# Attention and two MLPs on one core: the bias of the exponential from one VectorE operation, two loads on another queue, and a new order

## The chip, the cores and the metric

The kernel runs on one core of a Trainium2 chip. The metric is the device time of one launch, in microseconds (us). The kernel before was timed in three runs: 570.5, 571.86 and 574.29 us, median 571.86.

The core has five engines with an instruction queue each: TensorE (PE in the rows, with its weight loads as PEld), VectorE (DVE), ScalarE (ACT), GpSimd (POOL) and SyncE (SP, which here only issues DMA transfers). An engine works through its queue in order; between engines there are semaphores.

## The reference, cut to what matters

```python
q_rot, k_rot = rotate(q), rotate(k)          # 2 x 8 heads, 576 rows, 64 columns; cos/sin tables
scores = q_rot @ k_rot.T / sqrt(64)
scores = scores - max(scores, axis=-1)
attn = exp(scores)
attn = attn / (sum(attn, axis=-1) + 1e-9)
x = attn @ v                                 # heads side by side: 1152 tokens x 512
h = x @ w_in;  g = h * tanh(softplus(h));            y = g @ w_out     # 2048 wide
h = y @ w_in2; g = h * sigmoid(1.702 * h);           out = g @ w_out2  # 2048 wide
```

All of it is float32. The weights arrive as 64-bit floats.

## The kernel before, in words

The program has two parts. The first is attention, over 8 pairs of heads (4 for each of the 2 batch entries); the second is the two MLPs, whose matmuls follow one another without a pause. The change touches only the first part.

To keep float32 precision, numbers are split in a high and a low part, and products take three terms. For a pair, the rows 0 to 511 of q and k are rotated (`rope_ops`, two multiplications for each of q and k, on VectorE or GpSimd), transposed on TensorE (`turn`), and split by ScalarE (`high`) and VectorE (`low`) into the tile `qk`. The rows 512 to 575 of all four pairs of a batch entry lie in one tile, `rest`, and go through `rest_ops`. The scores of a pair are 9 tiles of 128 rows by 576 columns in PSUM, `st`, in a ring of three buffers. A score tile then goes through this chain:

- `s_max` (VectorE): the negated maximum of each row, into `nm[:, 0:1]`;
- `s_bias` (VectorE or ScalarE, as the planner chooses): `nm[:, 1:2] = nm[:, 0:1] * SCALE + LOGP`. LOGP is the logarithm of 2^14, by which the exponentials are scaled;
- `s_exp` (ScalarE): the exponential with that bias, and its row sum. The row sum is a second instruction, an accumulator read;
- a split into two float16 parts (`high`, `low`), and a transpose by DMA or on TensorE (`et`, which uses the same ring as `st`);
- the product with v on TensorE (`pv`), and a normalization (`xf`, `xh`, `xl`).

For v the greatest absolute value of each row is needed first: `v_max` (ScalarE), two activations with accumulator reads for two pairs of heads, whose main output goes to a tile that nobody reads, `junk`.

The order in which all this is issued is made by a planner when the program is built (class `Plan`): each step has a cost for each engine that may run it, the names that it needs and makes, the buffers that it holds, and a rank (`RANK`); the planner plays the program and takes the ready step of the lowest rank. It knows the buffers that it was told of, and `junk` is not among them. Where it sees TensorE waiting more than 0.2 us it puts matmuls whose result nobody uses (`keep_clock`, 128 x 192 in float16, called fillers below) in front of the next step. The order is thus fixed at build time, and the fillers too.

Of the kernel before, what the change touches and what calls it, by code (L numbers as in the profile page):

```python
# [11 lines left out]
F32 = mybir.dt.float32  # L12
# [3 lines left out]
AF = mybir.ActivationFunctionType  # L16
# [6 lines left out]
def kernel(  # L23
# [67 lines left out]
    idle = const.tile([128, 192], F16, name="idle")  # L91
    rtmp = {}
    rest = att.tile([128, 2, 2, NPAIR, 64], F32, name="rest", bufs=1)
    diag = att.tile([128, 2, NPAIR, 128], F32, name="diag", bufs=1)
# [20 lines left out]
    def load_rest(b, i, a):  # L115

        src = (q, k)[i][b].rearrange("(j a) s d -> a s j d", a=2)[a, MAIN:S]
        SP.dma_start(out=rest[64 * a:64 * a + 64, 0, i], in_=src)
# [65 lines left out]
    def rest_ops():  # L184

        s, t = (rest[:, j].rearrange("p i j d -> p (i j) d") for j in range(2))
        n = 2 * NPAIR
# [18 lines left out]
    def turn(p, m):  # L206
# [17 lines left out]
        else:  # L224
            PE.matmul(out=ps[:, 0:64], lhsT=diag[:, 1, p % NPAIR], rhs=pair_id, start=True, stop=True)
            PE.transpose(ps[:, 64:192], diag[:, 0, p % NPAIR], ident)
# [42 lines left out]
    def s_exp(p, n, st, nm):  # L269
# [3 lines left out]
        if (p, n // 2) not in ebuf:  # L273
# [5 lines left out]
            bias=nm[:, 1:2], scale=SCALE, accum_out=sums[p][:, n:n + 1],  # L279
# [366 lines left out]
    class Plan:  # L646
# [13 lines left out]
        PORT = {"rope", "rest", "high", "low", "v low", "xh", "xl", "w", "rr", "rw"}  # L660
# [149 lines left out]
        "rw": 2013.3, "rw DVE": 485.6, "rw POOL": 1292.9, "first": 282.5, "load q": -135.2, "load k": -17.6,  # L810
        "load rest": -720, "load v": 154.6, "load w": 1000.9, "rest": 437.3, "rope": -637.8, "turn": 410.7,
        "v max": 1129.4, "v high": -570.9, "v low": -441.3, "s": -323.6, "max": -880.6, "exp": -420.6,
        "high": -670.9, "low": -495.5, "pt": -314.5, "rc": 499.4, "rr": 1336.6, "rm": 157.8, "rb": 415.9,
        "pv": 512.1, "xf": 156.1, "xh": 414.9, "xl": 588.5, "w": 439.2, "u": -539.4, "rest DVE": 394.7,
        "rope POOL": -724, "high DVE": -1076.2, "low DVE": 586.6, "xh DVE": 489.8, "xl DVE": 503.9, "et": -283.5,
        "eh": 244.8, "el": 413.7, "v high ACT": 551.2, "w POOL": 477, "rr ACT": -503.1, "rr DVE": 449.3,
        "eh DVE": 489.8, "load sin": -726, "load cos": -435.1, "bias": 84, "bias ACT": 1271.3,
# [25 lines left out]
    def plan_rest(b):  # L843
        base, hold = 9 * NPAIR * b, [("rest", b)]
        for i in range(2):
            for a in range(2):
                add("SP", 0.65, (base, "load rest"), lambda i=i, a=a: load_rest(b, i, a), makes=("rest", b), holds=hold,
                    move=0.18, lead=1.2)
        ops = rest_ops()
        made = [("rest", b), "sin", "cos"]  # L850
        for j, f in enumerate(ops + ops[2:]):
            arg = (j - 2,) if j > 1 else ()
            add(None, dict(POOL=1.22, DVE=0.6), (base + j, "rest"), lambda eng, f=f, arg=arg: f(eng, *arg), needs=made,
                makes=("rest", b, j), holds=hold + [("diag", b)] * (j > 1))
            made = [("rest", b, j) for j in range(min(j, 1) + 1)]
# [15 lines left out]
    def plan_pair(p):  # L871
# [8 lines left out]
        for m in range(3):  # L880
            if m < 2:
                need, src = [("sw", p, m), ("st", p, m), "ident"], [("rtmp0", 2 * p + m), ("rtmp1", 2 * p + m)]
            else:
                need, src = [("rest", p // NPAIR, 2), ("rest", p // NPAIR, 3), "ident"], [("diag", p // NPAIR)]
# [28 lines left out]
        for at, n in enumerate(TILES[p]):  # L913
# [6 lines left out]
            else:  # L920
# [102 lines left out]
    add("SP", 0.48, (0, "load sin"), lambda: SP.dma_start(out=rsin.rearrange("p t d -> p (t d)"), in_=rope[:, 0:NSIN]),  # L1023
        makes="sin", move=0.46, lead=1.1)
    add("SP", 0.48, (0, "load cos"), lambda: SP.dma_start(out=rcos.rearrange("p t d -> p (t d)"), in_=rope[:, NSIN:]),
# [129 lines left out]
```

## Time and profile before

| | |
|---|---|
| runs before | 570.5, 571.86, 574.29 us; median 571.86 |
| the profiled execution | 572.92 us, of which its span is 571.1 |
| TensorE busy | 556.7 us, 97% of the span; fillers (L643) 292 matmuls |
| VectorE, ScalarE, GpSimd busy | 358.7, 281.5, 104.6 us |
| granted clock, mean | 0.997 |
| first matmul on scores | at 17.0 us |
| first matmul of the MLPs | at 166.3 us |

Busy time of an engine is the time in which at least one of its instructions ran. Matmuls are pipelined, so instructions overlap, and the start of one to the start of the next is less than its duration. Durations of VectorE overlap too, by some 0.07 us. A row of the trace names the line of the kernel, the engine, the operation and the tiles, output before input.

### The profile page before, as it was taken

The page shows a single profiled execution, that of the slowest core. Times are in us where ns is not written, and L with a number is a line of the kernel's source. Part 1 is how long each engine was busy: PE and PEld are TensorE (multiplying, and loading weights), DVE is VectorE, ACT ScalarE, POOL GpSimd, SP SyncE. Part 2 cuts the span into 40 slices and gives each one's busy share as a digit, 9 for nine tenths or more (in the row PEclk, how much of TensorE's full clock was granted, in tenths as well). Part 3 has the DMA queues.
Part 4 walks back from the last instruction along what each step waited for, and adds up shares of the span by engine and source line. Part 5 has one row for each costly group of instructions (what it writes and reads, how often), then busy time and mean ns, then how long its engine had stood idle before and what let it go on. Part 6 is the DMA issues. An engine that isn't in the chain of part 4 may idle for free.

```text
span 571.1 us, 9367 instructions
## 1 busy us (share of the span) xinstructions
PE 556.7 (97%) x3680; PEld 503.0 (88%) x3680; DVE 358.7 (63%) x657; ACT 281.5 (49%) x627; POOL 104.6 (18%) x95
## 2 busy tenths in 40 slices
PE   7889999999999999999999999999999999999997
PEld 7767777677789999999999999999988889998885
DVE  5888998989974977255896737757540237931031
ACT  2578988999855753122576313256520324752000
POOL 0758777666610000000000000000000000000000
PEclk9989999999999999999999999999999999999999
DMA  5497798769651433323443322323320034300032
GB/s 161 121 202 163 181 194 181 163 116 192 139 143 41 147 111 118 103 75 112 147 148 110 109 60 91 111 75 115 106 75 0 10 101 116 106 1 1 0 111 55
DMA packets 109356, 61.62 MB, mean 108 GB/s; under 512 B 75136, under 2 KB 106112, under 8 KB 109312
## 3 DMA queue, kind: packets, MB, share of 16 engines
q1 hardware_dynamic: 109312, 61.03, 40.7%
q8 instruction: 29, 0.48, 0.4%
q14 instruction: 15, 0.12, 0.1%
HBM read 40.96 MB, written 2.36 MB: 76 GB/s over the span
## 4 chain that ended last, share of the span: by engine, by line
PE 87%; DVE 7%; issue 2%; ACT 2%; SPq 1%; DMA 1%; DVEq 0%; ACTq 0%
PE h L534 31%; PE acc L601 15%; PE acc L615 15%; PE st L248 6%; PE pvps L371 5%; PE pvps L534 4%; PE pvps L601 2%; DVE nm L258 2%; PE pvps L615 2%; PE tps L219 2%; PE et L324 2%; ACT e L276 1%; PE pvps L643 1%; DVE rtmp L181 1%; DMA raw<-in_k_dram 1%
## 5 line engine op out<-in xcount | busy, mean ns | idle before, releaser
L534 PE MATMUL h<-x,whl 128*128 128x384 f32 x1008 | 178.6, 335 | 0.0
L534 PEld LDWEIGHTS h<-x,whl 128*128 128x128 f32 x1008 | 174.9, 188 | 0.8 <-issue 0.8
L465 DVE TENSOR_TENSOR whl<-wf,whl 128x512 fp32r<-128x512 f32 x63 | 43.6, 692 | 95.6 <-ACT whl L464 95.6
L615 PE MATMUL acc<-whl,g 128*128 128x512 f32 x384 | 88.9, 389 | 0.0
L601 PE MATMUL acc<-g,whl 128*128 128x384 f32 x504 | 88.6, 334 | 0.0
L601 PEld LDWEIGHTS acc<-g,whl 128*128 128x128 f32 x504 | 87.5, 188 | 0.0
L615 PEld LDWEIGHTS acc<-whl,g 128*128 128x128 f32 x384 | 72.1, 188 | 14.9
L571 DVE TENSOR_TENSOR g<-t,g 128x384 fp32r<-128x384 f32 x96 | 53.0, 553 | 30.1 <-ACT g L581 30.1
L464 ACT ACTIVATE whl<-wf 128x512 fp32r<-128x512 f32 x64 | 40.1, 627 | 59.3 <-DVE wf L483 40.1
L248 PE MATMUL st<-qk 64*128 64x288 f32 (+1 forms) x432 | 59.7, 325 | 2.9 <-ACT e L276 2.7
L295 POOL TENSOR_TENSOR p<-e,p 128x576 f16<-128x576 f32 x43 | 57.5, 1346 | 20.8 <-issue 11.0
L580 ACT ACTIVATE t<-h 128x384 f32<-128x384 f32 x84 | 40.6, 483 | 40.6 <-PE h L534 40.4
L258 DVE TENSOR_REDUCE nm<-st 128x1 f32<-128x576 f32 x72 | 53.1, 749 | 6.8 <-PE st L248 6.0
L248 PEld LDWEIGHTS st<-qk 64*128 64x128 f32 (+1 forms) x432 | 41.4, 186 | 17.1 <-issue 10.8
L581 ACT ACTIVATE g<-t 128x384 fp32r<-128x384 f32 x96 | 50.6, 527 | 3.1
L276 ACT ACTIVATE e<-st,nm 128x576 f32<-128x576 f32 x64 | 46.9, 734 | 3.1 <-DVE nm L265 2.1
L480 DVE SCALAR_TENSOR_TENSOR wf<-wraw,wf 128x512 int32<-128x512 int32 x64 | 45.2, 706 | 1.6
L483 DVE SCALAR_TENSOR_TENSOR wf<-wraw,wf 128x512 int32<-128x512 int32 x64 | 44.1, 689 | 1.3
L371 PE MATMUL pvps<-pt,vh 128*64 128x256 f16 (+1 forms) x480 | 37.9, 293 | 0.0
L371 PEld LDWEIGHTS <-vh 128*64 128x64 f16 x480 | 23.5, 110 | 9.0 <-issue 7.1
L643 PE MATMUL pvps<-idle 128*128 128x192 f16 x292 | 30.2, 255 | 1.0 <-DVE idle L1014 1.0
L1096 DVE TENSOR_TENSOR acc<-acc,acc 128x512 f32<-128x512 f32 x8 | 5.5, 687 | 37.1 <-PE acc L615 37.1
(102 smaller groups left out, 538.8 us busy)
## 6 DMA issues: line engine op xcount, KB each, us to landing
wraw<-in_moe_w_in_dram SPq DMA_DIRECT2D x32, 512.0 KB, 3.5
wraw<-in_moe_w_out_dram SPq DMA_DIRECT2D x32, 512.0 KB, 3.4
raw<-in_v_dram SPq DMA_DIRECT2D x4, 512.0 KB, 5.1
raw<-in_q_dram SPq DMA_DIRECT2D x3, 512.0 KB, 4.0
raw<-in_k_dram SPq DMA_DIRECT2D x3, 512.0 KB, 5.3
out_dram<-acc SPq DMA_DIRECT2D x10, 128.0 KB, 2.4
out_dram<-acc SPq DMA_DIRECT2D x4, 256.0 KB, 2.4
raw<-in_q_dram SPq DMA_DIRECT2D x2, 256.0 KB, 3.2
```

Source lines behind the costliest of these rows:

```text
L248: PE.matmul(out=st[:, g, 0:HALF], lhsT=t[r, ql, c0:c0 + 128], rhs=t[r, kl, KC + HALF * g:KC + HALF * g + HALF], start=(i == 0), stop=(i == 2),
L258: DVE.tensor_reduce(out=nm[:, 0:1], in_=st[:, :, 0:HALF], axis=AX.XY, op=ALU.max, negate=True)
L276: ACT.activation(out=ebuf[p, n // 2][:, n % 2, :].rearrange("p (g s) -> p g s", g=2), in_=st[:, :, 0:HALF], func=AF.Exp, bias=nm[:, 1:2], ...
L295: eng.tensor_tensor(out=t[1], in0=src, in1=t[0], op=ALU.subtract)
L371: PE.matmul(out=ps[64 * a:64 * a + 64, 0:W], lhsT=w[:, vl, a, kb, :], rhs=pt[:, KB * (2 * a + pl) + kb, :], start=(n == 0), stop=(n == len ...
L480: lambda: DVE.scalar_tensor_tensor(out=t, in0=hi, scalar=-0x40000000, in1=t, op0=ALU.bitwise_and, op1=ALU.bitwise_or),
L483: lambda: DVE.scalar_tensor_tensor(out=t, in0=lo, scalar=29, in1=t, op0=ALU.logical_shift_right, op1=ALU.bitwise_or),
L534: PE.matmul(out=ps[:, 0:UN], lhsT=w[:, wl, 128 * kk:128 * kk + 128], rhs=src[:, xl, kk, cols(u)], start=(kk == 0 and (wl, xl) == X_LAST[0] ...
L571: DVE.tensor_tensor(out=gl, in0=t, in1=f32(gh), op=ALU.subtract)
L581: ACT.activation(out=gh, in_=t, func=AF.Copy)
L601: PE.matmul(out=ps[:, 0:UN], lhsT=w[:, wl, 128 * f:128 * f + 128], rhs=g[:, gl, 4 * half + f, cols(u)], start=(half == 0 and f == 0 and (w ...
L615: PE.matmul(out=ps, lhsT=g[:, gl, f, 128 * t:128 * t + 128], rhs=w[:, wl, :], start=(f == 0 and (gl, wl) == TERMS[0]), stop=(f == FC - 1 a ...
```

## The change

It does four things.

- `s_max` and `s_bias` become one `tensor_tensor_reduce`: to each score a constant (`shift`, minus LOGP / SCALE) is added, the sum is multiplied by -SCALE, and the minimum over the row is kept, which is the bias that the exponential wants. The 576 products themselves are written as float16 to `junk`, the tile that `v_max` also writes. The built program has two VectorE instructions for it, the main one and one on `nm` alone.
- The cos and sin tables and the rows 512 to 575 of q and k of the first batch entry are loaded by transfers issued from ScalarE's queue, no longer from SyncE's.
- The tiles `rest` and `diag` are laid out with the pair outermost, and for the first batch entry the pair 0 is computed apart from the pairs 1 to 3.
- `RANK` and a few planner costs are new, so the whole attention part comes in another order.

```diff
-    rest = att.tile([128, 2, 2, NPAIR, 64], F32, name="rest", bufs=1)
-    diag = att.tile([128, 2, NPAIR, 128], F32, name="diag", bufs=1)
+    rest = att.tile([128, 2, NPAIR, 2, 64], F32, name="rest", bufs=1)
+    diag = att.tile([128, NPAIR, 2, 128], F32, name="diag", bufs=1)
...
     def s_max(st):
-        nm = att.tile([128, 2], F32, tag="nm", name="nm", bufs=4)
-        DVE.tensor_reduce(out=nm[:, 0:1], in_=st[:, :, 0:HALF], axis=AX.XY, op=ALU.max, negate=True)
+
+        nm = att.tile([128, 1], F32, tag="nm", name="nm", bufs=4)
+        DVE.tensor_tensor_reduce(
+            out=junk[:, 0:S].rearrange("p (g s) -> p g s", g=2), in0=st[:, :, 0:HALF], in1=shift.unsqueeze(2).to_broadcast([128, 2, HALF]), scale=-SCALE,
+            scalar=3.0e38, op0=ALU.add, op1=ALU.min, accum_out=nm,
+        )
         return nm
-
-    def s_bias(nm, eng):
-        if eng is ACT:
-            ACT.activation(out=nm[:, 1:2], in_=nm[:, 0:1], func=AF.Copy, scale=SCALE, bias=LOGP)
-        else:
-            DVE.tensor_scalar(nm[:, 1:2], nm[:, 0:1], SCALE, LOGP, op0=ALU.mult, op1=ALU.add)
...
-            bias=nm[:, 1:2], scale=SCALE, accum_out=sums[p][:, n:n + 1],
+            bias=nm, scale=SCALE, accum_out=sums[p][:, n:n + 1],
...
-        "rw": 2013.3, "rw DVE": 485.6, "rw POOL": 1292.9, "first": 282.5, "load q": -135.2, "load k": -17.6,
+        "rw": -414.4, "rw DVE": -540.2, "rw POOL": -100, "first": 1741.3, "load q": -421.8, "load k": -518.5,
...
     def plan_rest(b):
         base, hold = 9 * NPAIR * b, [("rest", b)]
+        e, q = (SP, "SP") if b else (ACT, "ACT")
         for i in range(2):
             for a in range(2):
-                add("SP", 0.65, (base, "load rest"), lambda i=i, a=a: load_rest(b, i, a), makes=("rest", b), holds=hold,
+                add(q, 0.65, (base, "load rest"), lambda i=i, a=a: load_rest(e, b, i, a), makes=("rest", b), holds=hold,
                     move=0.18, lead=1.2)
...
+        for j0, j1 in ((0, NPAIR),) if b else ((0, 1), (1, NPAIR)):
+            ops = rest_ops(slice(j0, j1))
...
-            add("DVE", 0.665, (g, "max"), lambda n=n: d.update({("m", n): s_max(d["s", n])}), needs=[("s", g)],
+            add("DVE", 0.72, (g, "max"), lambda n=n: d.update({("m", n): s_max(d["s", n])}), needs=[("s", g)],
                 makes=("max", g), holds=[s_at, ("nm", g)])
-            add(None, dict(DVE=0.069, ACT=0.094), (g, "bias"), lambda eng, n=n: s_bias(d["m", n], eng),
-                needs=[("max", g)], makes=("bias", g), holds=[("nm", g)])
-            add("ACT", 0.717, (g, "exp"), lambda n=n: s_exp(p, n, d["s", n], d["m", n]), needs=[("bias", g)],
+            add("ACT", 0.717, (g, "exp"), lambda n=n: s_exp(p, n, d["s", n], d["m", n]), needs=[("max", g)],
...
+    DVE.memset(shift, -LOGP / SCALE)
...
-    add("SP", 0.48, (0, "load sin"), lambda: SP.dma_start(out=rsin.rearrange("p t d -> p (t d)"), in_=rope[:, 0:NSIN]),
+    add("ACT", 0.48, (0, "load sin"), lambda: ACT.dma_start(out=rsin.rearrange("p t d -> p (t d)"), in_=rope[:, 0:NSIN]),
         makes="sin", move=0.46, lead=1.1)
```

The order changes at many places. Three of them matter for what follows.

The first is the head of SyncE's queue, which issues the first loads (`raw_85` is q, `raw_86` k and `raw_87` v of the kernel before):

```order
L1023 DMA rsin<-in_rope_dram 128x320
L118 DMA rest<-in_q_dram 64x4x64 x2
L118 DMA rest<-in_k_dram 64x4x64 x2
L1025 DMA rcos<-in_rope_dram 128x320
L110 DMA raw_85<-in_q_dram 128x2x256 x2
L110 DMA raw_86<-in_k_dram 128x2x256 x2
L110 DMA raw_87<-in_v_dram 128x4x256
```

In the changed kernel SyncE begins with k, q and v at once (there `raw_87` is k, `raw_86` q and `raw_88` v), and the six small transfers stand at the head of ScalarE's queue, in front of its table load, and `v_max` (L132) has come in front of the first splits (L233):

```order
L1026 DMA rsin<-in_rope_dram 128x320
L1028 DMA rcos<-in_rope_dram 128x320
L119 DMA rest<-in_q_dram 64x4x64 x2
L119 DMA rest<-in_k_dram 64x4x64 x2
L132 ACT_TABLE_LOAD
L132 ACTIVATE junk,vs<-raw_88 128x640 x2
L233 ACTIVATE qk<-tps 128x512 x2
L233 ACTIVATE qk<-pvps 128x192
```

Before, one split stood in front of `v_max`, and two behind it.

The third place is VectorE's queue some 80 rows into the changed program, around the second call of `v_max`. The rows are those of the change, with the engines that each waits for (Activation is ScalarE; a wait for DVE is one for an earlier instruction of the same engine):

```order
L294 TENSOR_TENSOR pr<-er,pr 128x576 [waits DMAHW4_49,DMAHW5_49,Activation_49,Pool_49]
L260 ISA junk,nm<-st,shift 128x576 [waits DVE_49,PE_49]
L260 ISA nm 128x1
L260 ISA junk,nm<-st,shift 128x576 [waits DVE_49,PE_49,Activation_49]
L260 ISA nm 128x1
```

In the program, `v_max` stands between these two uses of `junk`, and on ScalarE it waits for the first of them:

```order
L392 ACTIVATE rb_700<-rps,vs 128x256 [waits PE_49]
L132 ACTIVATE junk,vs<-raw_88 128x640 [waits DMAHW7_49,DMAHW0_49,DVE_49]
L132 ACTIVATE junk,vs<-raw_88 128x640 [waits Activation_49]
L275 ACTIVATE e,sums<-st,nm 128x576 [waits PE_49,Pool_49]
L275 ACTIVATE e,sums<-st,nm 128x576 [waits DVE_49]
```

Before, `L131 ACTIVATE junk` waited for no VectorE instruction that writes `junk`, since there was none, and no `L258 TENSOR_REDUCE` waited for it. Each reduction of a score tile, one instruction before (72 of them, and 40 of the 72 biases on VectorE, 32 on ScalarE), is two now, 144 in all.

Counted over the whole program, the change also issues 209 fillers in place of 292 (of those in front of the first score matmul 65 in place of 93), runs ten rotations fewer on VectorE (eight with cos, two with sin) and ten more on GpSimd, and does three `et` copies, six `xl` subtractions and two `pr` subtractions more on VectorE. Of the `rest` operations VectorE had seven of 512 columns; it now has five, all smaller, and GpSimd has the others. The second, third and fourth call of `v_max` each stand between two uses of `junk` on VectorE; behind the second call the next use follows at once, behind the other two one other VectorE operation of 512 or 640 columns lies between.

## Rows read from the trace of the kernel before

**Rows 1.** Windows: us, busy of PE, PEld, DVE, ACT, POOL; clock; DMA; GB/s.
```profile
0.00:5.00 5.00, 3.99 (x30) 3.81 (x31) 1.71 (x8) 1.28 (x1) 1.38 (x10) 1.00 0.33 79
5.00:10.00 5.00, 3.37 (x37) 2.98 (x36) 2.59 (x4) 0.00 (x0) 0.00 (x0) 1.00 0.93 268
...
300.00:400.00 100.00, 100.00 (x579) 100.00 (x578) 65.62 (x120) 40.44 (x78) 0.00 (x0) 1.00 0.31 96
```

**Rows 2.** Windows, same columns: the start, one stretch, the rest of attention.
```profile
0.00:17.00 17.00, 13.34 (x121) 11.93 (x121) 10.83 (x23) 4.36 (x8) 1.47 (x11) 1.00 0.62 172
...
92.00:110.00 18.00, 17.74 (x166) 12.79 (x165) 16.40 (x33) 16.38 (x43) 14.43 (x14) 1.00 0.81 187
...
17.00:166.00 149.00, 142.25 (x1368) 108.91 (x1368) 134.16 (x253) 126.89 (x327) 102.68 (x85) 0.99 0.77 165
```

**Rows 3.** Windows of the fillers (L643) alone: busy of PE and PEld.
```profile
0.00:17.00 17.00, 9.91 (x93) 9.10 (x93) 1.00 0.62 172
17.00:166.00 149.00, 20.33 (x199) 16.06 (x199) 0.99 0.77 165
```

**Rows 4.** Timeline of PE: start, duration; two blocks of fillers.
```profile
27.81 1.74 PE L643 MATMUL pvps<-idle 128*128 128x192 f16 x19
...
155.05 1.91 PE L643 MATMUL pvps<-idle 128*128 128x192 f16 x21
```

**Rows 5.** Timeline, the start: loads, rotation, v_max, first score matmuls.
```profile
1.19 1.40 SPq L118 DMA_DIRECT2D rest<-in_q_dram  x2
...
4.59 0.95 SPq L110 DMA_DIRECT2D raw<-in_q_dram  x2
...
7.69 0.69 DVE L177 TENSOR_TENSOR rtmp<-raw,rsin 128x512 f32<-128x512 f32 x1 [1.17 <-DMA raw<-in_q_dram]
...
12.70 0.74 ACT L131 ACTIVATE junk<-raw 128x640 f16<-128x640 f32 x1 [1.44 <-DMA raw<-in_v_dram]
...
17.00 1.46 PE L248 MATMUL st<-qk 64*128 64x288 f32 x15
```

**Rows 6.** Groups by form: line, operation, count | busy, mean ns | idle before.
```profile
L258 DVE TENSOR_REDUCE nm<-st 128x1 f32<-128x576 f32 x72 | 53.1, 749 | 6.8 <-PE st L248 6.0 <-ACT e L276 0.2
...
L181 DVE TENSOR_TENSOR rtmp<-raw,rcos 128x512 f32<-128x512 f32 x12 | 11.3, 944 | 0.6 <-PE tps L219 0.6
...
L235 DVE TENSOR_TENSOR qk<-tps,qk 128x512 fp32r<-128x512 f32 x16 | 10.8, 680 | 1.8 <-ACT qk L232 1.8
...
L265 DVE TENSOR_SCALAR nm<-nm 128x1 f32<-128x1 f32 x40 | 5.9, 149 | 0.7
```

**Rows 7.** Timeline of one score tile: reductions, bias, exponential and its accumulator read.
```profile
84.14 1.42 DVE L258 TENSOR_REDUCE nm<-st 128x1 f32<-128x576 f32 x2 [0.27 <-PE st L248]
...
85.59 0.15 DVE L265 TENSOR_SCALAR nm<-nm 128x1 f32<-128x1 f32 x1
85.67 1.02 DVE L156 SCALAR_TENSOR_TENSOR vh<-raw,vs,vh 128x640 f16<-128x640 f32 x1
85.68 0.73 ACT L276 ACTIVATE e<-st,nm 128x576 f32<-128x576 f32 x1
...
86.31 0.20 ACT L276 ACTIVATION_READ_ACCUMULATOR e<-st,nm 128x1 f32 x1
...
86.40 0.74 ACT L276 ACTIVATE e<-st,nm 128x576 f32<-128x576 f32 x1
```

**Rows 8.** Timeline of ScalarE: one call of v_max in mid program.
```profile
99.88 0.72 ACT L131 ACTIVATE junk<-raw 128x640 f16<-128x640 f32 x1
...
101.37 0.19 ACT L131 ACTIVATION_READ_ACCUMULATOR junk<-raw 128x1 f32 x1
```

**Rows 9.** Windows, columns as in Rows 1: a wait of TensorE and its clock.
```profile
36.00:38.00 2.00, 0.70 (x6) 0.56 (x8) 2.00 (x6) 1.30 (x4) 0.00 (x0) 1.00 1.33 155
38.00:40.00 2.00, 2.00 (x18) 1.36 (x16) 1.47 (x3) 2.00 (x6) 1.45 (x2) 0.61 0.93 195
40.00:42.00 2.00, 2.00 (x12) 1.69 (x12) 0.82 (x2) 1.43 (x5) 1.17 (x1) 0.54 1.04 351
```

More of the change, by code (lines that the diff above doesn't have):

```diff
@@ L182, in rope_ops, with rest_ops @@
         return swapped, straight
-    def rest_ops():
-        s, t = (rest[:, j].rearrange("p i j d -> p (i j) d") for j in range(2))
-        n = 2 * NPAIR
+    def rest_ops(js):
+        s, t = (rest[:, i, js].rearrange("p j i d -> p (j i) d") for i in range(2))
+        n = 2 * (js.stop - js.start)
         def swapped(eng):
@@ L224, in turn @@
         else:
-            PE.matmul(out=ps[:, 0:64], lhsT=diag[:, 1, p % NPAIR], rhs=pair_id, start=True, stop=True)
-            PE.transpose(ps[:, 64:192], diag[:, 0, p % NPAIR], ident)
+            PE.matmul(out=ps[:, 0:64], lhsT=diag[:, p % NPAIR, 1], rhs=pair_id, start=True, stop=True)
+            PE.transpose(ps[:, 64:192], diag[:, p % NPAIR, 0], ident)
             c0, c1 = KC + MAIN, QC
@@ L659 @@
         WINDOW, BUSY = 10.24 / 3, 3400
-        PORT = {"rope", "rest", "high", "low", "v low", "xh", "xl", "w", "rr", "rw"}
+        PORT = {"rope", "rest", "first rest", "high", "low", "v low", "xh", "xl", "w", "rr", "rw"}
         def __init__(self):
@@ L809 @@
     RANK = {
-        "rw": 2013.3, "rw DVE": 485.6, "rw POOL": 1292.9, "first": 282.5, "load q": -135.2, "load k": -17.6,
[L811 to L817, printed above, removed]
+        "rw": -414.4, "rw DVE": -540.2, "rw POOL": -100, "first": 1741.3, "load q": -421.8, "load k": -518.5,
+        "load rest": 404.2, "load v": -155.7, "load w": 2071, "rest": -678.3, "rope": 1998.5, "turn": -1992.8,
+        "v max": 2001.6, "v high": 2045.4, "v low": -951.4, "s": -757.6, "max": -587.8, "exp": -419.9,
+        "high": 2428.6, "low": -328.2, "pt": 1223.5, "rc": -411.5, "rr": -87, "rm": -372.7, "rb": 1744.8,
+        "pv": 1873.8, "xf": -1174.7, "xh": -65, "xl": 2152, "w": 2384.5, "u": 1911.9, "first rest": -763.2,
+        "first rest DVE": 208.9, "rest DVE": 2564.8, "rope POOL": -340.4, "high DVE": -485.6, "low DVE": 1853.8,
+        "xh DVE": -672.1, "xl DVE": 1730.2, "et": 16.2, "eh": 1537.4, "el": -884.5, "v high ACT": -85.1,
+        "w POOL": -443.6, "rr ACT": -466.4, "rr DVE": 1995.9, "eh DVE": -583.6, "load sin": -997.5,
+        "load cos": -213.4,
     }
@@ L844, in plan_rest @@
         base, hold = 9 * NPAIR * b, [("rest", b)]
+        e, q = (SP, "SP") if b else (ACT, "ACT")
         for i in range(2):
             for a in range(2):
-                add("SP", 0.65, (base, "load rest"), lambda i=i, a=a: load_rest(b, i, a), makes=("rest", b), holds=hold,
+                add(q, 0.65, (base, "load rest"), lambda i=i, a=a: load_rest(e, b, i, a), makes=("rest", b), holds=hold,
                     move=0.18, lead=1.2)
[L849 to L855, printed above, removed]
+        for j0, j1 in ((0, NPAIR),) if b else ((0, 1), (1, NPAIR)):
+            ops = rest_ops(slice(j0, j1))
+            made, kind = [("rest", b), "sin", "cos"], "rest" if b or j0 else "first rest"
+            n = (j1 - j0) / NPAIR
+            for j, f in enumerate(ops + ops[2:]):
+                arg = (j - 2,) if j > 1 else ()
+                add(None, dict(POOL=0.12 + 1.1 * n, DVE=0.07 + 0.53 * n), (base + j0 + j, kind),
+                    lambda eng, f=f, arg=arg: f(eng, *arg), needs=made,
+                    makes=[("rest", NPAIR * b + k, j) for k in range(j0, j1)], holds=hold + [("diag", b)] * (j > 1))
+                made = [("rest", NPAIR * b + j0, j) for j in range(min(j, 1) + 1)]
     def plan_v(ps):
```

11 lines of the change are left out of this document (6 added, 5 removed).

## The prediction

> **What bounds the kernel now.** I read the windows first, to see where time can be won at all. In the MLPs TensorE is busy all of every 100 us [rows 1], and the change takes nothing from them; only what lies before the first MLP matmul counts, some 166 us. In the first 17 us there is no score matmul; in the other 149 TensorE is busy 142.25, VectorE 134.16 (90%), ScalarE 126.89 (85%) and GpSimd 102.68 [rows 2]. TensorE's figure is too good, so I read the fillers next: 9.91 us of it in the start and 20.33 later are matmuls that nobody needs [rows 3]. The reader should see two kinds of stretch. From 92 to 110 TensorE is busy 17.74 of 18.00 without a filler: there it is the bound itself, and nothing that eases VectorE shows. Elsewhere it waits for VectorE and ScalarE, behind fillers or idle. What can be won is at most fillers and idle time: 30.2 us of fillers and 17.0 - 13.34 + 149.0 - 142.25 = 10.4 us idle. The third view is the timeline: the start, one score tile, and one call of v_max. Real TensorE work is the same after the change, so I count what happens to its waits.
>
> **The start.** SyncE spends 0.65 to 0.7 us on issuing each 64 KB piece of `rest`, and reaches the first load of q only at 4.59 [rows 5]. In these first 5 us the transfers run at 79 GB/s, in the next 5 at 268 [rows 1]: issuing is the limit, not moving. With both queues issuing from the beginning, and some 2 us until the first bytes move, the first 5 us would carry 3 x 268 = 804 KB in place of 5 x 79 = 395, so all that follows lands about 409 / 268 = 1.5 us earlier. v now comes first on ScalarE: v_max began at 12.70 [rows 5] and would begin at about 11.2; it takes 1.68 us from the first activation to the end of the last read [rows 8]. Behind it come two splits of 512 columns and one of 192 with their subtractions, some 2.1 us by the spacings of such operations (680 ns a subtraction [rows 6]). That puts the first score matmul at 15.0, not 17.00: **-2.0 us**. The six transfers on ScalarE cost nothing, since it has only 4.36 us of work in these 17 [rows 2]; were they slow there, the table load behind them would still be done before 11. The bounds: -3.4 if v is no gate (VectorE then has some eight operations of 0.6 between q's landing and the first subtraction), -0.5 if the two queues' transfers delay one another and v lands only little earlier. The order's 28 fillers fewer before the first score matmul say -2.4, inside the bounds.
>
> **The later fillers.** 144 stand behind the first score matmul in place of 199. One costs (1.91 - 1.74) / 2 = 0.085 us [rows 4]; 55 x 0.085 = **-4.7 us**, if the waits that they stood for are gone. So I ask whether the engines are really relieved. VectorE: the new operation reads 576 columns from PSUM and a constant from SBUF and writes float16. Nearest is the subtraction `qk`, also PSUM and SBUF in, 680 ns for 512 columns with no stretching by GpSimd over 16 of them, so about 750 for 576, no more than the reduction's 749 [rows 6]. Reductions start 1.42 - 0.75 = 0.67 apart [rows 7]. The small second instruction is not in the trace on VectorE. Nearest is ScalarE's accumulator read, which starts 0.10 before its parent ends (85.68 + 0.73 against 86.31) and is followed 0.09 later by the next [rows 7]; a bias on VectorE is followed after 0.08. So the pair takes 0.67 + 0.08 = 0.75 by the nearest row. Below it cannot go under 0.67 + 0.06; above, if the read starts as the dependent bias did, 0.03 after the end (84.14 + 1.42 against 85.59), it is 0.75 + 0.03 + 0.08 = 0.86. At 0.75, 72 x 0.08 = 5.8 us come, 40 biases x 0.08 = 3.2 go. Ten rotations go, at 944 ns (stretched, since GpSimd's operations and these hold each other up; I take the sine ones alike): 9.4 us. Seven `rest` operations give way to five smaller, at least 2 x 0.68 = 1.4. Eleven other operations come, each at most as long as a reduction: at most 8.2. VectorE's sum: at most +2.6 - 9.4 - 1.4 + 8.2 = 0, and nearer -3, as most of the eleven are shorter. ScalarE loses 32 biases, some 0.1 each, 3 us, and gets about as much back as half of that. GpSimd gets ten rotations, about 13 us, and gives up as many shorter ones; it had 46 us free [rows 2]. Per tile the step from maximum to exponential is shorter by some 0.15, as no second engine comes between. So the relief is there, small, and about the size of the fillers taken out.
>
> **A new wait.** `junk` ties VectorE and ScalarE together. Around the second call of v_max, VectorE's next use of `junk` stands directly behind the use that v_max waits for: VectorE stops for 1.68 us [rows 8], with all of its later work behind it, and the next tile's exponential waits for that. Around the third and fourth call one operation of about 0.7 lies between, and 1.0 is left. That is at most 1.7 + 1.0 + 1.0 = 3.7. At least 0.3 each, 1.0, because ScalarE has an exponential of 0.73 left to run when v_max ends, and only what the next tile needs beyond it (0.75 + 0.15, and a handover) is lost. I take the middle, **+2.0**. The pair's 0.75 against the 0.72 that the order was laid out for: 72 x 0.03 = 2.2 on VectorE, a quarter on the path: **+0.5**.
>
> The sum against the profiled execution's 572.9: 572.9 - 2.0 - 4.7 + 2.0 + 0.5 = 568.7. The median of the three runs lies 1.1 below that execution, which makes 567.6; I say **568.0**.
>
> **The rivals.**
>
> 1. *The waits on `junk` are covered.* ScalarE and TensorE have other work at these places, so +2.0 becomes nothing. And at 36 to 38 TensorE was busy 0.70 of 2.00 us, after which the granted clock fell to 0.61 and 0.54 for 4 us [rows 9], between its levels of 2.4 and 1.2 GHz; that took 0.78 + 0.92 = 1.7 us. In a new order this wait may not be there. 568.0 - 2.0 - 1.0 = 565. For it: only 1.7 of 166 us hang on the clock, at one place. Against: a new order has its own such place.
> 2. *The fillers go, the waits stay.* 55 fillers fewer with TensorE idle in their place gain nothing, and idle stretches may cost clock, as above. Only the start remains: 571.9 - 2.0 + 1 = 571. For it: 92 to 110 shows TensorE as its own bound, and VectorE's relief is only about 2% of its work.
> 3. *The second queue does not help.* If the transfers of the two queues hold each other up, v lands as late as before: the start gains 0, and the rest -4.7 + 2.0 + 0.5 = -2.2, so 570. Against it: issuing took SyncE 3.9 us of the first 4.6 [rows 5] while little moved [rows 1]. The Trainium skill (DMA: Bandwidth & Descriptors, section Issuing engines are not separate DMA queues) is on this rival's side: issuing from several engines only saves the issuing time, which is usually small against the transfer.
> 4. *Slower: the pair is two full instructions.* If the read starts only when the main instruction has ended and the next only when the read has, a tile costs 0.75 + 0.03 + 0.15 = 0.93, 0.26 more than a reduction now. 72 x 0.26 = 18.7, less the 3.2 of biases: +15.5, while some 3 to 6 go elsewhere. VectorE would have to be busy some 145 of 149 us, and it had 14.8 free, most of it waits that stay. I take half of the +15.5 as time: 568.0 + 7.8 + 3 for the splits and exponentials that come late = 579. It decides from about 0.80 a tile on, where the pair's growth (72 x 0.13, less 3.2) eats what the rotations give back. Against it: the bias after a reduction, and the reads on ScalarE, overlap [rows 7]. The Trainium skill (VectorE: DVE Perf Modes, section The DRAIN you can't avoid) says that the next operation does not start until the pipe is empty, and its Rules for kernel authors advise against fusing for speed, for fewer operations instead; 144 in place of 112 is more. Followed to the letter that gives this rival; the trace disagrees where a `vh` starts 0.07 before the bias in front of it ends, 85.67 against 85.74 [rows 7].
>
> **How the numbers follow.** The forecast has 0.40, its own range 565.8 to 570.4; rival 1 has 0.31, rival 2 0.12, rival 3 0.07, rival 4 0.10. More than 1% faster (about what can be told from no change here) is below 566.1: rival 1 and a sixth of the forecast, 0.31 + 0.07 = 0.38. Within 1%: 0.33 + 0.12 + 0.07 = 0.52. Slower: 0.10. The range, 563.0 to 574.0, leaves out rival 4 and the lower third of rival 1.
>
> **What the changed profile would show.** First score matmul near 15.0, and v_max in front of both splits, from about 11; if v_max starts after 12, the start's term is wrong. The new VectorE operation at 740 to 760 ns, started again 0.75 apart; at 0.80 and more rival 4 is on. VectorE idle for about 1.7 us before a score operation released by ScalarE's `junk` row, once, and 1.0 twice; without these rows the +2.0 falls. TensorE idle from 17 us on no more than 7 to 8 us; more means rival 2. The first MLP matmul would come later than the 4.2 us suggest, since the last products of attention now stand in front of it all; the end is what counts. A clock below 0.9 in any two windows of 2 us would make the prediction wrong by about 1 us each.

## The result, and the profile after

The changed kernel takes 568.14 us (median of 6 runs, 567.39 to 569.08) against 573.34 for the kernel before beside it (6 runs, 570.5 to 574.77). The ratio is 0.9915, interval 0.9891 to 0.9939: 4.9 us faster (the medians lie 5.2 apart). The forecast was 568.0 us, 563 to 574. The sum is right; three of its terms are not, and their errors cancel.

The page of the changed kernel (line, engine, operation, count | busy, mean ns | idle before, by releaser), the new operation and the fillers:

```profile
span 565.2 us, 9206 instructions
...
PE 547.8 (97%) x3597; PEld 497.3 (88%) x3597; DVE 355.3 (63%) x686; ACT 278.4 (49%) x599; POOL 112.8 (20%) x99
...
L260 DVE CUSTOM_DVE_ANT_1 junk<-st,shift 128x576 f16<-128x576 f32 x72 | 54.1, 752 | 10.4 <-ACT junk L132 4.4
...
L642 PE MATMUL pvps<-idle 128*128 128x192 f16 x209 | 24.8, 268 | 2.9 <-DVE xf L402 1.8
```

The profiled execution took 567.39 us. TensorE is busy 547.8 of 565.2, so idle 17.4; before it was 556.7 of 571.1, idle 14.4. Of the 5.9 us between the spans, 5.5 are fillers (30.25 [rows 3], now 24.8), 3.5 are real matmuls that took less time (1.7 of it the clock fall of [rows 9], which this execution does not have), and 3.0 came back as idle time.

Windows of the changed kernel, columns as in [rows 1], and in the second fence the fillers alone, as in [rows 3]:

```profile
0.00:5.00 5.00, 3.98 (x26) 3.79 (x27) 1.72 (x9) 0.00 (x0) 1.38 (x10) 1.00 0.62 186
5.00:10.00 5.00, 4.39 (x38) 4.08 (x36) 3.10 (x5) 0.00 (x0) 0.00 (x0) 1.00 1.08 258
...
0.00:17.00 17.00, 12.22 (x96) 11.09 (x97) 10.90 (x24) 4.47 (x9) 4.65 (x13) 1.00 0.64 170
...
17.00:166.00 149.00, 140.35 (x1360) 108.24 (x1358) 134.32 (x289) 125.41 (x304) 108.11 (x87) 1.00 0.87 165
```

```profile
0.00:17.00 17.00, 8.71 (x65) 7.91 (x65) 1.00 0.64 170
17.00:166.00 149.00, 16.08 (x144) 11.87 (x144) 1.00 0.87 165
```

Against [rows 1, 2]: the first 5 us move 186 GB/s in place of 79, as the prediction had it, yet the start hardly gains. From 17 to 166 VectorE is busy as long as before (134.32 against 134.16), but this window is not the same work: in the changed kernel its last 2.62 us belong to the MLPs. From the first score matmul to the first MLP matmul VectorE is busy 132.15 us now (16.67 to 163.38) and was busy 134.43 before (17.00 to 166.30). TensorE idles 8.65 us in place of 6.75.

The start in the timeline (start, duration; what ended the idle time before), against [rows 5]:

```profile
3.97 1.81 ACTq L119 DMA_DIRECT2D rest<-in_k_dram  x2
...
6.77 1.29 DVE L178 TENSOR_TENSOR rtmp<-raw,rsin 128x512 f32<-128x512 f32 x2 [3.97 <-DMA raw<-in_q_dram]
...
10.73 0.29 DVE L192 TENSOR_TENSOR rest<-rest,rsin 128x128 f32<-128x128 f32 x1 [0.87 <-issue]
...
10.94 1.49 DVE L182 TENSOR_TENSOR rtmp<-raw,rcos 128x512 f32<-128x512 f32 x1
10.94 1.28 ACT L132 ACT_TABLE_LOAD   x1 [10.94 <-DMA raw<-in_v_dram]
11.85 1.71 POOL L182 TENSOR_TENSOR rtmp<-raw,rcos 128x512 f32<-128x512 f32 x1
12.24 0.74 ACT L132 ACTIVATE junk<-raw 128x640 f16<-128x640 f32 x1
12.35 1.35 DVE L196 TENSOR_TENSOR rest<-rest,rcos 128x128 f32<-128x128 f32 x1
...
14.23 0.58 DVE L200 TENSOR_TENSOR diag<-rest 64x128 f32<-64x128 f32 x2
...
14.86 0.43 PE L226 MATMUL pvps<-pair_id,diag 128*128 128x64 f32 x2 [2.97 <-DVE diag L200]
...
16.67 0.96 PEld L249 LDWEIGHTS st<-qk 64*128 64x128 f32 x13 [0.17 <-issue]
```

v lands at 10.94 (forecast: about 11.2). But ScalarE's table load waits for v too, so `v_max` begins at 12.24. And a second gate is shut: the rows of `rest` can be used only at 10.73, after q and k (this row names no releaser; the same row from one queue, in experiment 6, names `rest`), and two of VectorE's operations behind that take 1.49 and 1.35 us while GpSimd works beside them. TensorE stands 2.97 us until `diag` is made. The first score matmul comes at 16.67, 0.3 earlier than before.

The same timeline, VectorE and ScalarE: two tiles of the first pair, and the second call of `v_max`, against [rows 7, 8]:

```profile
18.02 0.75 DVE L260 CUSTOM_DVE_ANT_1 junk<-st,shift 128x576 f16<-128x576 f32 x1
18.69 0.08 DVE L260 DVE_READ_ACCUMULATOR2_ANT nm<- 128x1 f32 x1
18.91 0.76 DVE L260 CUSTOM_DVE_ANT_1 junk<-st,shift 128x576 f16<-128x576 f32 x1
...
44.82 0.08 DVE L260 DVE_READ_ACCUMULATOR2_ANT nm<- 128x1 f32 x1
44.82 0.41 DVE L402 TENSOR_TENSOR xf<-pvps,rb 128x256 f32<-128x256 f32 x1
...
48.12 0.19 ACT L132 ACTIVATION_READ_ACCUMULATOR junk<-raw 128x1 f32 x1
...
48.34 0.76 DVE L260 CUSTOM_DVE_ANT_1 junk<-st,shift 128x576 f16<-128x576 f32 x1 [1.76 <-ACT junk L132]
```

The read starts 0.67 after its parent, and another operation starts with it, so the pair costs no more than the reduction did. Only where the next new operation stands directly behind does it start 0.22 after the read, 0.89 after the one before. It writes the same `junk`, but in the one such gap that the profile puts down to a wait it names the read (`nm`, 0.2 us), so what holds it is open. And VectorE stands 1.76 us until `v_max` has left `junk`; there are three such stops, 4.4 us in all (the group's row above).

### The profile page after: what moved, and what is told of

Same layout as the page of the kernel before. It is cut to its first block, busy times and chain, and to the rows that moved or that the text cites. A ratio compares the mean times of both kernels' runs of the same rounds, so it can differ in the third digit from the quotient of the medians.

```text
span 565.2 us, 9206 instructions
## 1 busy us (share of the span) xinstructions
PE 547.8 (97%) x3597; PEld 497.3 (88%) x3597; DVE 355.3 (63%) x686; ACT 278.4 (49%) x599; POOL 112.8 (20%) x99
## 4 chain that ended last, share of the span: by engine, by line
PE 76%; ACT 2%; DVE 2%; issue 1%; POOL 1%; DVEq 0%
PE h L533 31%; PE acc L600 15%; PE acc L614 15%; PE pvps L533 4%; PE st L249 2%; PE pvps L600 2%; PE pvps L370 2%; PE pvps L614 2%; ACT e L275 1%; DVE pt L294 1%; DVE junk L260 1%; PE rps L386 0%; ACT p L288 0%; PE tps L220 0%; POOL rtmp L182 0%
## 5 line engine op out<-in xcount | busy, mean ns | idle before, releaser
L260 DVE CUSTOM_DVE_ANT_1 junk<-st,shift 128x576 f16<-128x576 f32 x72 | 54.1, 752 | 10.4 <-ACT junk L132 4.4
L249 PE MATMUL st<-qk 64*128 64x288 f32 (+1 forms) x432 | 58.3, 322 | 2.3 <-ACT e L275 1.1
L642 PE MATMUL pvps<-idle 128*128 128x192 f16 x209 | 24.8, 268 | 2.9 <-DVE xf L402 1.8
```

Source lines behind the costliest of these rows:

```text
L249: PE.matmul(out=st[:, g, 0:HALF], lhsT=t[r, ql, c0:c0 + 128], rhs=t[r, kl, KC + HALF * g:KC + HALF * g + HALF], start=(i == 0), stop=(i == 2),
L260: DVE.tensor_tensor_reduce(out=junk[:, 0:S].rearrange("p (g s) -> p g s", g=2), in0=st[:, :, 0:HALF], in1=shift.unsqueeze(2).to_broadcast( ...
```

## The experiments

Each was timed beside the kernel before. That spread from 570.3 to 575.9 us (medians 572.5 to 572.8), the kernels of the new order by 1.3 to 2.4 us each, but 3.9 with `rest` before the tables and 4.5 without later fillers. So kernels of the new order are best compared with each other by their medians, where a few tenths say nothing, and with the kernel before by the ratio. For the profiled executions this table splits the span at the first score matmul:

| kernel | median us | ratio, interval | first score matmul | rest of the span |
|---|---|---|---|---|
| before | 573.34 | 1 | 17.00 | 554.1 |
| changed | 568.14 | 0.9915, 0.9891 to 0.9939 | 16.67 | 548.5 |
| changed, again | 568.43 | 0.9932, 0.9906 to 0.9958 | 17.75 | 549.2 |
| own tile | 565.66 | 0.9885, 0.9855 to 0.9915 | 17.64 | 545.9 |
| early table load | 568.78 | 0.9929, 0.9903 to 0.9955 | 16.54 | 548.3 |
| both of these | 566.08 | 0.9888, 0.9858 to 0.9918 | 16.91 | 546.1 |
| both, v behind `rest` | 566.69 | 0.9904, 0.9881 to 0.9926 | 15.93 | 549.2 |
| both, `rest` before tables | 569.16 | 0.9942, 0.9919 to 0.9965 | 19.64 | 548.8 |
| changed, one queue | 568.84 | 0.9937, 0.9918 to 0.9956 | 17.86 | 548.5 |
| changed, two operations | 568.53 | 0.9940, 0.9919 to 0.9961 | 17.54 | 548.9 |
| two operations, one queue | 569.70 | 0.9961, 0.9944 to 0.9977 | 18.33 | 549.0 |
| before, one operation | 573.23 | 1.0012, 0.9996 to 1.0027 | 17.38 | 553.4 |
| before, second queue | 571.76 | 0.9994, 0.9977 to 1.0010 | 17.34 | 553.9 |
| changed, no later fillers | 574.50 | 1.0031, 1.0011 to 1.0051 | 18.05 | 554.5 |

**1. The changed kernel again.** No edit; it stands beside the next ones.

> The changed kernel once more, as the measure for the three that run beside it. Every theory: 568.1 us, plus or minus 0.8.

568.43 us. Its profiled execution took 569.07, 1.7 more than the first one, with the same order and the same wait. The windows show why: this one (first fence, the window of the wait and what follows), and the first execution (second fence):

```profile
12.00:14.00 2.00, 0.00 (x0) 0.00 (x0) 2.00 (x3) 1.96 (x4) 1.74 (x2) 1.00 0.05 17
14.00:16.00 2.00, 0.95 (x5) 0.80 (x6) 1.96 (x5) 1.20 (x4) 0.00 (x0) 0.62 0.76 253
16.00:18.00 2.00, 2.00 (x11) 1.67 (x11) 1.80 (x3) 0.48 (x2) 1.27 (x1) 0.50 0.72 215
18.00:20.00 2.00, 2.00 (x15) 1.93 (x15) 1.40 (x3) 0.45 (x1) 1.54 (x2) 0.50 0.14 47
```

```profile
14.00:16.00 2.00, 0.95 (x7) 0.73 (x8) 1.96 (x5) 1.24 (x3) 0.00 (x0) 1.00 0.84 252
16.00:18.00 2.00, 2.00 (x22) 1.73 (x20) 1.45 (x4) 0.60 (x1) 1.59 (x2) 1.00 0.71 230
```

TensorE idled 3.20 us here and 2.97 there before `diag`. Here the granted clock then fell to 0.50, 1.2 GHz, and was back by 22 us; there it stayed at 1.00, 2.4 GHz.

**2. The new operation's products in a tile of their own.**

```diff
-    junk = att.tile([128, 2 * KB * 64], F16, name="junk", bufs=1)
+    junk = att.tile([128, 2 * KB * 64], U8, name="junk", bufs=1)
+    waste = att.tile([128, S], U8, name="waste", bufs=1)
...
-            out=junk[:, 0:S].rearrange("p (g s) -> p g s", g=2), ...
+            out=waste.rearrange("p (g s) -> p g s", g=2), ...
```

> The changed kernel, but the products of the new VectorE operation go to a tile of their own, so that it and v_max no longer wait for one another; to make room both throw-away tiles hold 8-bit numbers. Order and fillers are the same. Theory A (the prediction's +2.0): VectorE's three waits for v_max (4.4 us in the changed kernel) are gone and 1.0 to 3.7 us come back, about 2, so some 566. Rival (the waits lie beside other work): the three waits are gone and the time is the same within 0.5 us. In both, the new operation stays at 740 to 760 ns.

565.66 us, 2.8 less than the changed kernel beside it, and with the early table load of the next experiment 566.08 against 568.78, again 2.7. The same place in the timeline of this kernel:

```profile
45.55 0.08 DVE L262 DVE_READ_ACCUMULATOR2_ANT nm<- 128x1 f32 x1
45.55 0.41 DVE L404 TENSOR_TENSOR xf<-pvps,rb 128x256 f32<-128x256 f32 x1
...
47.22 0.08 DVE L262 DVE_READ_ACCUMULATOR2_ANT nm<- 128x1 f32 x1
47.44 0.76 DVE L262 CUSTOM_DVE_ANT_1 waste<-st,shift 128x576 uint8<-128x576 f32 x1
```

The stop of 1.76 us is gone; 0.22 behind the read stay, where one such operation directly follows another. The operation takes 752 ns as before, so the smaller products did nothing, and what was won is the wait. This is the best kernel measured, 0.9885 of the kernel before.

**3. The table load early.** One activation on one column behind the six transfers, so that the table is there when v lands.

```diff
+    warm = const.tile([128, 1], F32, name="warm")
...
+        if eng is ACT and i and a:
+            ACT.activation(out=warm, in_=idle[:, 0:1], func=AF.Abs)
```

> The changed kernel with one more ScalarE activation of one column, right behind the six transfers on its queue, so that the table load (1.28 us) is done before v lands. Theory A (ScalarE is the gate of the start): the splits begin 1.3 us earlier, the first score matmul at 15.4 in place of 16.67, and 1.3 us are won, some 566.8. Rival (VectorE's queue is a second gate: the rotation of rows 512 to 575 ends at 14.8, since these rows land late, and the subtractions stand behind it): v_max ends 1.3 us earlier, the first score matmul at 16.3 to 16.7, and at most 0.4 us are won.

568.78 us: nothing won. The timeline of this kernel:

```profile
10.81 0.74 ACT L135 ACTIVATE junk<-raw 128x640 f16<-128x640 f32 x1 [3.79 <-DMA raw<-in_v_dram]
...
14.73 0.43 PE L229 MATMUL pvps<-pair_id,diag 128*128 128x64 f32 x2 [2.76 <-DVE diag L203]
...
16.54 1.05 PE L252 MATMUL st<-qk 64*128 64x288 f32 x11
```

`v_max` comes 1.4 us earlier, the first score matmul 0.13: the table load did hold `v_max` up, but `v_max` was not the gate any more. `rest` and VectorE's queue were. Together with the own tile:

> Both edits together: the own tile, and the early table load. Theory A: the two add up, 568.1 - 2.0 - 1.3 = 564.8. Rival (neither is on the path): 567.6 to 568.6.

566.08 us, as the own tile alone.

**4. v from ScalarE's queue, behind `rest`** (with both edits above), so that `rest` lands first. The two loads of v are taken out of SyncE's queue.

```diff
         if eng is ACT and i and a:
+            load((0, 1), 2, ACT)
+            load_v_rest((0, 1), ACT)
             ACT.activation(out=warm, in_=idle[:, 0:1], func=AF.Abs)
...
```

> Own tile, early table load, and the first v issued from ScalarE's queue behind rest, so that rest lands before it. Theory A (VectorE waits 0.9 us for rest at 9.9, and GpSimd's part of rest then collides with VectorE's at 11 to 13.6): rest lands by 9, diag is done at 12.5 to 13.5 in place of 14.8, TensorE's idle of 3 us before it is halved and its clock does not fall, first score matmul at 15 to 16, 564 to 565. Rival (v lands later, and v_max stands in front of the splits): first score matmul at 16.5 or later, 566.

TensorE's wait before `diag` fell from 2.97 to 2.03 us and the first score matmul came at 15.93, but the time is 566.69, 0.6 more than without the edit (the intervals of the ratios overlap). In its windows the clock fell nonetheless, and once more later:

```profile
14.00:16.00 2.00, 1.82 (x14) 1.27 (x14) 1.93 (x4) 0.33 (x1) 0.00 (x0) 0.87 0.80 268
16.00:18.00 2.00, 2.00 (x14) 2.00 (x15) 0.92 (x2) 0.60 (x1) 1.49 (x2) 0.50 0.68 238
```

At 90 to 94 it stood at 0.65 and 0.50. So 0.7 us at the start was won against the changed kernel, and was not to be seen in the time.

**5. `rest` before the tables on ScalarE's queue** (with the own tile and the early table load).

```diff
+    first_loads = [lambda i=i, a=a: load_rest(ACT, 0, i, a) for i in range(2) for a in range(2)] + [
+        ... the sin table, the cos table, the activation for the table load
...
```

> Own tile and early table load, and on ScalarE's queue the four pieces of rest stand in front of the two tables (same six transfers). Theory A (the start's gate is rest, which landed at 10.7 behind tables, k, q and v, so that diag was done at 14.8 and TensorE stood idle for 3.0 us): rest lands by 7, its rotation is not held up by GpSimd's at 11 to 13.6, diag is done by 12.5, first score matmul at 14.0 to 15.0, no idle of 3 us and no fall of the clock at 14 to 20 us; 2 us less than with the own tile alone (565.7), so 563.5. Rival (v and v_max gate the start anyhow): first score matmul at 16 or later, 565 to 566.

569.16 us, 3.1 more than without. Neither theory had this. The timeline:

```profile
4.16 0.36 ACTq L1030 DMA_DIRECT2D rsin<-in_rope_dram  x1
...
6.21 0.34 ACTq L1031 DMA_DIRECT2D rcos<-in_rope_dram  x1
...
10.60 0.30 PE L223 MATMUL tps<-ident,rtmp 128*128 128x128 f32 x1 [3.75 <-DVE rtmp L181]
```

The tables were issued behind `rest` at 4.16 and 6.21, and TensorE now stands 3.75 us for the first rotation in place of `diag`: the gate moved to the tables. Its clock was 0.50 from 12 to 18.

**6. One queue.** The changed kernel with the six transfers from SyncE again, and the kernel before with them from ScalarE.

```diff
-... lambda i=i, a=a: load_rest(e, b, i, a), ...
+... lambda i=i, a=a: load_rest(SP, b, i, a), ...
-... lambda: ACT.dma_start(out=rsin.rearrange("p t d -> p (t d)"), in_=rope[:, 0:NSIN]),
+... lambda: SP.dma_start(out=rsin.rearrange("p t d -> p (t d)"), in_=rope[:, 0:NSIN]),
...
```

> The changed kernel with the six transfers issued from SyncE again, in the order that the planner gives (sin, k, cos, k, rest, q, q, rest, v, rest, v's rest, rest). The prediction's term: the second queue is worth 2 us, so 570.4. Theory A (rest is the gate and comes last in either case): rest lands some 0.5 to 1 us later than from the second queue, first score matmul at 17 to 17.7, 568.4 to 569.4.

> The kernel before, its own order, in which the tables and the first rest are issued from ScalarE's queue and nothing else changes. The prediction's term for the start (issuing is the limit, so all lands about 1.5 us earlier): first score matmul at 15.0 to 15.5 in place of 17.0, 1.5 to 2 us faster than before. Theory A (the rest transfers are slow beside those of q, k and v): rest lands at 9 to 10.7 in place of 5.8, and since its rotation is VectorE's first operation in this order, all rotations wait for it: first score matmul at 18 to 20, 1 to 3 us slower than before.

The changed kernel loses 0.4 us without the second queue (568.84), which is not clear of noise; the kernel before gains nothing with it (571.76, ratio 0.9977 to 1.0010): its `rest` comes at 7.49 in place of 5.83, and its first score matmul at 17.34. A third pair, with two operations (experiment 7), loses 1.2 without the second queue, 569.70 against 568.53, with intervals that overlap. The new order from one queue:

```profile
11.36 1.28 ACT L132 ACT_TABLE_LOAD   x1 [11.36 <-DMA raw<-in_v_dram]
11.53 0.29 DVE L192 TENSOR_TENSOR rest<-rest,rsin 128x128 f32<-128x128 f32 x1 [0.91 <-DMA rest<-in_k_dram]
```

So v lands 0.4 and `rest` 0.8 later than from two queues (in the second execution of the changed kernel v came at 11.24, so some of that is chance), although the last piece of `rest` is issued by 7.81 in place of 5.78: 2.0 us saved in issuing are 0.8 at landing. And the first 5 us move 157 GB/s from one queue in the new order, and 194 from two in the old one: either change alone lifts the 79, and neither brings the start forward by the 2.0 us of the prediction. The Trainium skill (DMA: Bandwidth & Descriptors, section Issuing engines are not separate DMA queues) says that another issuing engine saves only the issuing time, usually little against the transfer; these runs agree, with 0 to 1.2 us.

**7. Two operations in the new order, and that from one queue.** The reduction and the bias apart again, both on VectorE; with the edits of experiment 6 as well, only the order is left of the change.

```diff
-        DVE.tensor_tensor_reduce(...)
+        DVE.tensor_reduce(out=nm[:, 0:1], in_=st[:, :, 0:HALF], axis=AX.XY, op=ALU.max, negate=True)
+        DVE.tensor_scalar(nm[:, 1:2], nm[:, 0:1], SCALE, LOGP, op0=ALU.mult, op1=ALU.add)
```

> The changed kernel, its order, fillers and both queues, but each score tile by a reduction and a bias on VectorE again (all 72 biases there), so nothing but v_max writes junk. Theory A (the order brings the gain; the one operation saves 0.1 to 0.2 us a tile, and its waits on junk cost 2.8): two instructions started 0.86 apart in place of 0.68 to 0.89, some 5 us more on VectorE, a third of it on the path, less 2.8: 567 to 568. Rival (the one operation is what makes this order fast): 571 or more. Rival (it is worth nothing even here): as with the own tile, 565.7.

> As the kernel with two operations, and the six transfers issued from SyncE as well: what is left of the change is the new order, its fillers and the split of rest. Theory A (the order is the change): within 1 us of the kernel with two operations, and 4 us or more faster than before. Rival (order, queue and operation are each worth a third): 570 to 572.

Two operations: 568.53, the same as the changed kernel. The groups by form of this kernel, and its window:

```profile
L260 DVE TENSOR_REDUCE nm<-st 128x1 f32<-128x576 f32 x72 | 53.9, 748 | 2.8 <-PE st L249 2.6
...
L261 DVE TENSOR_SCALAR nm<-nm 128x1 f32<-128x1 f32 x72 | 11.1, 154 | 2.5
```

```profile
17.00:166.00 149.00, 140.95 (x1356) 108.31 (x1355) 139.69 (x288) 124.41 (x302) 108.68 (x87) 1.00 0.87 164
```

VectorE is busy 5.4 us longer in this window than in the changed kernel, and has no stop for `junk`. Against the own tile, 565.66, the single operation is worth 2.9 us; in the changed kernel the stops take 2.8 of it back. The order alone gives 569.70, 2.8 us less than before by the medians, 1.3 to 3.2 by the ratio, although its first score matmul is 1.3 later: behind that matmul it is 5.1 us shorter in the profiled executions. Its own is the fastest of its twelve; by the medians, 2.8 and 1.3, it is 4.1.

**8. One operation in the old order**, products in a tile of their own.

```diff
+        DVE.tensor_tensor_reduce(out=waste.rearrange("p (g s) -> p g s", g=2), ...)
...
-        if eng is ACT:
-            ACT.activation(out=nm[:, 1:2], in_=nm[:, 0:1], func=AF.Copy, scale=SCALE, bias=LOGP)
-        else:
-            DVE.tensor_scalar(nm[:, 1:2], nm[:, 0:1], SCALE, LOGP, op0=ALU.mult, op1=ALU.add)
+        pass
```

> The kernel before, its own order and fillers, with the one operation in place of reduction and bias and nothing in place of the 72 biases; its products go to a tile of their own. What the operation is worth by itself. Theory A (VectorE gets 72 x 0.08 less 40 x 0.08 = 2.6 us more, ScalarE 3.2 less, and each tile's exponential may start 0.15 earlier, all between waits): 0 to 2 us faster than before. Rival (the fused operation is the change's gain): 4 to 6 us faster. Rival (144 instructions on VectorE in place of 112 cost their price): 2 us slower or more.

573.23 us, ratio 0.9996 to 1.0027: by itself the operation is worth nothing there. The old order with its 292 fillers stands, and TensorE idles 7.0 us from 17 to 166 in place of 6.75: what VectorE saves ends in waits.

**9. No fillers behind the first score matmul.**

```diff
-                    if n:
+                    if n and not begun:
...
+                    begun = begun or last == "s"
```

> The changed kernel without its 144 fillers behind the first score matmul. Theory A (a filler only stands in for a wait; the prediction counted 0.085 us for each on the ground that the wait goes with it): the same within 1 us as long as the clock holds, with 12 to 16 us more of idle TensorE in 17 to 166 us; where the clock falls to half for 4 us, 2 us more. Rival (fillers hold up the matmul behind them): 2 to 6 us faster.

574.50 us, 6 more than the changed kernel. The windows of this kernel:

```profile
17.00:166.00 149.00, 135.15 (x1155) 102.25 (x1155) 129.67 (x278) 123.04 (x296) 108.21 (x87) 0.89 0.82 161
...
28.00:42.00 14.00, 12.62 (x63) 10.49 (x64) 10.86 (x27) 11.70 (x29) 11.49 (x10) 0.51 0.77 139
```

With 16.08 us of fillers fewer, TensorE idles 13.85 us in place of 8.65 and its clock falls in five stretches (the first, at 14 to 22, is also in the second execution of the changed kernel), from 28 to 42 to 0.51. Its 1155 matmuls in this window are busy 135.15 us; the changed kernel's 1216 real ones were busy 124.27. So without fillers the clock is lost, and that costs more than the room they leave is worth. What fewer fillers would give with the clock kept, this run does not show.

## Why the prediction came out right, and where it was wrong

**The start (-2.0): wrong, -0.3.** The step that failed is "v now comes first on ScalarE: v_max began at 12.70 and would begin at about 11.2". v came at 10.94, near the figure, but not for the reason given: from one queue it came at 11.36, so of the 1.8 us that it is earlier at most 0.4 are the second queue's, and the rest is the order's. The table load that "would still be done before 11" stood behind the same wait, and the mark that I had set myself, v_max after 12, was passed (12.24). The early table load shows that this was not even the error that counted: with v_max at 10.81 the first score matmul came at 16.54. Not in the sum was that `rest`, which no longer comes first, gates `diag`: now it can be used at 10.73. In the kernel before (its table load, its first user, and `rest`):

```profile
0.73 1.28 ACT L232 ACT_TABLE_LOAD   x1 [0.73 <-PEq L1140]
...
5.83 0.69 DVE L191 TENSOR_TENSOR rest<-rest,rsin 128x512 f32<-128x512 f32 x1 [3.04 <-DMA rest<-in_k_dram]
...
10.66 0.60 ACT L232 ACTIVATE qk<-tps 128x512 fp32r<-128x512 f32 x1 [8.65 <-PE tps L219]
```

There the load had not waited with its user, and `rest` was ready at 5.83. The lower bound of the term, -0.5, was nearer; in the second execution, where the clock fell, the first score matmul came at 17.75, later than before.

**The fillers and the relief (-4.7): near in size, for another reason.** The order alone shortens what lies behind the first score matmul by 4.1 to 5.1 us. VectorE's relief is there in the changed kernel, 2.3 us in its own stretch where "nearer -3" was said, but it does not carry the gain: the order alone is shorter with VectorE busy 138.75 us from 17 to 166, more than before. The relief is small: the ten rotations are gone, but other operations came, and some are stretched where GpSimd works beside them (it is busy 108.11 us in place of 102.68). The groups by form of VectorE, from 17 to 166, of the kernel before and then of the changed one (its first row is the small second instruction of the new operation):

```profile
L409 DVE TENSOR_TENSOR x<-xf,x 128x256 fp32r<-128x256 f32 x2 | 1.0, 518 | 0.2 <-ACT x L289 0.2
```

```profile
L260 DVE DVE_READ_ACCUMULATOR2_ANT nm<- 128x1 f32 x72 | 5.9, 82 | 0.0
...
L408 DVE TENSOR_TENSOR x<-xf,x 128x256 fp32r<-128x256 f32 x5 | 4.3, 868 | 0.0
```

The same subtraction takes 868 ns on the mean in place of 518. That the order wins by when things are ready is what is left, and was not shown step by step. Experiment 9 shows that leaving fillers out is no gain by itself; that the 55 fewer are a result of the order and no cause fits it, but was not tested with the clock kept. Of the 5.1 us, 1.7 are the clock fall at 36 to 42 [rows 9], which the new order does not have there; in most of the executions of that order there is one between 12 and 22 instead, as in the second of the changed kernel. How the rest is spread over the steps of the new order was not taken apart.

**The wait through `junk` (+2.0): right in kind, too small, +2.8.** The three stops are there, 4.4 us in place of 3.7, the longest 1.76 where 1.7 was said. More of them reaches the end than I took: experiment 2 gives 2.8 and, with the early table, 2.7.

**The pair (+0.5): nothing.** The operation takes 752 ns (forecast 740 to 760) and its read 82; the next one starts 0.67 to 0.68 later, not 0.75; directly behind another, 0.89. I had counted its gain into the fillers and given it no term of its own: it is 2.9 us in the new order (experiments 2 and 7), nothing in the old (8). In the changed kernel it pays for the `junk` wait, and that is why the two operations take the same time.

So behind the first score matmul there stand -5.1, -2.9 and +2.8 in place of -4.7, +2.0 and +0.5; the span there fell by 4.9 and 5.6 us in two executions, where -2.2 was forecast. That is some 3 us too little, against 1.7 too much at the start (2.75 in the second execution): that the sum came out is luck. Nor did the 1.1 us hold that were taken off for the median of three runs: the median of six, 573.34, lies 0.4 above the profiled execution.

Part of the gain is the clock's, which is in rival 1 and in no term of the sum. Of the 65 executions of the kernel before timed beside the experiments, the 21 with a mean granted clock of 0.999 or 1.0 took 570.3 to 572.1 us (medians 570.6 to 571.3), the others, down to 0.991, 572.0 to 575.9. The changed kernel took 567.4 at 0.998, 567.7 to 568.7 at 0.996 and 0.997, and 569.1 at 0.994. With little or no fall on either side, some 3 to 4 of the 4.9 us are left, an estimate from these times.

**The rivals.** Rival 1 named what the own tile then did: without the stops 566 was its figure ahead of the clock, 565.66 was measured. Rival 2 is there in part: TensorE's idle time from 17 us on is 8.65, over the 7 to 8 that I had allowed, so of the 4.25 us of fillers that went there 1.9 stayed as waits. Rival 3 has the start's size, not its reason: the second queue brings 0 to 1.2 us, but v lands 1.8 us earlier, not as late as before. Rival 4 is wrong: the next operation starts with the read. The rule of the Trainium skill behind it (VectorE: DVE Perf Modes, section The DRAIN you can't avoid: the next operation waits until the pipe is empty) is given there with an exception that the prediction left out: "A next op that is not held starts earlier". These rows fit the exception; the one gap that looks like the rule, 0.22, stands where the next new operation directly follows the read. The first MLP matmul came with all the products of attention in front of it, as expected, at 163.38 in place of 166.3.

## What to carry to other kernels

A scratch tile that nobody reads still orders its writers: when an operation gets one, give it its own, since two engines that share it stop each other. Before a start is shortened, list every transfer and every queue that the first real matmul needs; speeding up one gate shows nothing while a second opens at the same time, and look whether a table load stands behind the wait of its first user (it did here, and did not before). When an order is laid out anew together with an operation, run each alone: here the order gave 2.8 us, the second queue 0 to 1.2, the operation nothing in the old order and 2.9 in the new one, if its scratch tile is its own.

## What had not been expected of the hardware

- One program has two starts. After 2.97 us without a matmul the clock stayed at 2.4 GHz in one execution, after 3.20 it fell to 1.2 GHz in another, and with the own tile it fell after 2.97 as well; of the eleven profiled executions with the new order two show no fall before 22 us, these with waits of 2.97 and 2.76. With the wait at 2.03 (experiment 4) it fell too. Between the two executions of the changed kernel lie 1.7 us.
- Transfers of `rest` land late: the last was issued by 5.78, and the rows could be used at 10.73, while the first 5 us moved 186 and the next 258 GB/s. The time that issuing takes is no longer the limit there.
- On ScalarE's queue the cos table was issued 2.05 us after the sin table, 4.16 and 6.21, though issuing itself takes 0.36 (experiment 5). In the changed kernel SyncE was done with issuing q at 2.73 and issued v only at 4.51. What held them is not known; in the kernel before SyncE issued its first loads, up to 7.74, one behind the other.
